# Moving the load and transform steps of batches 1 to 4 in a global filter kernel, and reordering the filter spreads in its opening

## The chip, the cores and the metric

The kernel runs on one core of a Trainium2 chip. The engines of the core work side by side and wait for each other through semaphores: TensorE (matrix multiplies; PE in the profile, PEld for its weight loads), VectorE (DVE), ScalarE (ACT), GpSimd (POOL) and SyncE (SP), which here only issues DMA transfers. The metric is the device time of one execution in microseconds. Each engine executes its instructions in the order in which the program issued them, so an instruction that waits holds all that stand behind it on that engine.

## The reference

Eight batches of 3072 rows by 256 columns go through a global filter (a real FFT along the rows, a product with a complex filter, the inverse FFT), and every resulting row through a small network of two matrices, a maximum and an output matrix.

```python
X = np.fft.rfft(x, axis=1)               # x: 8 x 3072 x 256
Y = X * (filt_r + 1j * filt_i)[None]     # 1537 x 256 each
y = np.fft.irfft(Y, n=3072, axis=1)
h1 = y @ w1                              # 256 x 1024
h2 = y @ w2
out = np.maximum(h1, h2) @ w_out         # 1024 x 256
```

## The kernel before

**The transform.** 3072 is split into 128 times 24. Stage f1 multiplies x with a table of 128 points (`C1`) into `at`. That goes out to DRAM (`ad`) and comes back in another order as `bt`. Stage f2 works in eight groups: it multiplies `bt` with the table `U` (px, L469), multiplies the result with the filter `F` on VectorE (pq, L474) and transforms back with `VP` and `VQ` (pz, L447). ScalarE copies pz into `zt`, and each pair of groups goes to DRAM as `zd` by two writes (L456). `z_read` brings `zd` back as `zr` in two halves (L429), and `s4` multiplies `zr` with `G1` (py, L580) into `yt`, the rows that the network takes.

**The network.** The maximum of two products is computed as the relu of a difference plus the second: `moe_h` multiplies with `Wd`, which is w1 - w2 (L610), and clips the result, mostly on ScalarE. `moe_o` multiplies with `M`, which is w2 times w_out (L630), and adds the clipped part times `Wo` (L635). There are 48 tiles of 512 rows, six for each batch. Half a megabyte goes out for each tile through POOL's queue (L642).

**Folded loads.** From batch 2 on, x is loaded in six pieces a batch, each by two DMAs on SP's queue (`load_p`, L395). Two POOL operations (`fold_x`, L402) add and subtract the halves of a piece into `xd`. `f1_half` (L410) transforms a piece and issues its write of `ad` on SP. The eight reads of `f1_read` (L423) then bring the batch back as `bt`. All DMAs of loads, `ad`, `bt`, `zd` and `zr` are issued on SP, in the order of the program: an issue that waits holds the later ones.

**The order of the work.** The main loop at the end has 48 tiles of eight steps each; step `8 * tt + j` issues `moe_h(tt, j)`, then `moe_o(tt - 1, j)`, then what the dictionary `todo` holds for this step, in the order in which it was planned, and in one step of each tile `s4(tt + 1)`: in its fifth step (j = 4), but in the last tile of a batch at j = 6 (of the first batch at j = 7). `plan` fills `todo`: `plan_f2(n, steps, z1, z0)` gives the nine calls of f2 for batch n and the steps of its two z reads, and `plan_x(n, steps)` gives the loads of batch n and, 12 steps later, the folds. `spaced` makes rows of steps. So the numbers in these calls are a timetable written by hand. The generator `gen_f2(b)` also holds f1 of the next batch: `units` names the calls that begin with an `f1_half`. For batch 1 these are the third to the eighth, which start with piece 3; for the others the first, second, fourth, fifth, seventh and eighth, which start with piece 0. The `zd` writes are issued in the third, fifth, seventh and ninth call. `in_f2` names steps in which ScalarE takes all clippings; outside of them VectorE takes those of j = 1 and j = 5.

**The opening.** Before the loop, batch 0 is transformed without the way through DRAM, while the tables and the filter are made. `expand_f(g, ri, E)` spreads the filter's rows of group `g` (`ri` 0 the real part, 1 the imaginary) over the partitions: eight matmuls with `Sel` (L131, L134), and copies into `F` by engine `E`. On VectorE these are two copies (L141) out of two banks of the "px" ring, which has four; on ScalarE one copy (L514) out of a double bank of the "pa" ring, which has two and is used by `first_s1`, pz and pw as well. `first_t1` (L505) transposes a group of f1's result, `first_s2` (L521, L530) makes its products with `F`, of which in five rounds ScalarE and POOL make one of the two, and `first_s3` (L548) transforms back, two rounds later. `fix_f` (L306, L307) is three POOL operations that put the rows of frequency zero into group 0, after the DMAs of `patch_f0`. `order` is the order of the groups: 1, 2, 3, 4, 5, 0, 6, 7.

Of the kernel before, what the change touches and what calls it, by code (L numbers as in the profile page):

```python
# [29 lines left out]
def kernel(  # L30
# [26 lines left out]
    V, S, G, TE = nc.vector, nc.scalar, nc.gpsimd, nc.tensor  # L57
# [30 lines left out]
    def bank2(shape, dtype, name, tag=None):  # L88
        if tag is None:
            ring.append(ring.pop(0))  # L90
            tag = ring[-1]
        return p2.tile(shape, dtype, tag=tag, name=name)
# [5 lines left out]
    def load_x(b, c):  # L98
        t_ = xpool.tile([128, 4, D], BF16, tag="xb", name="xb")
        src = x[b].rearrange("(p n) d -> p n d", n=N2)  # L100
        G.dma_start(out=t_, in_=src[:, 4 * c:4 * c + 4, :])
        xb[b, c] = t_
# [17 lines left out]
    def expand_f(g, ri, E, sp=0):  # L120
        if E is V:
            pf = [p2.tile([128, 2, D], FP32, tag="px", name="pf", bufs=4) for _ in range(2)]
        else:
            p_ = bank2([128, 2, 2, D], FP32, "pf")
            pf = [p_[:, b] for b in range(2)]
        fs = Fs[ri]
        spin(pf[0].rearrange("p u d -> p (u d)"), sp)
        for b in range(2):
            for c in range(2):
                m = 4 * b + c  # L130
                TE.matmul(pf[b][64 * c:64 * c + 32], Sel[:, m], fs[:, 2 * g:2 * g + 2], start=True, stop=True)  # L131
                p0 = 64 * c + 32
                if g:
                    TE.matmul(pf[b][p0:p0 + 32], Sel[:, 7 - m], fs[:, 16 - 2 * g:14 - 2 * g:-1], start=True, stop=True)  # L134
                else:
                    TE.matmul(pf[b][p0:p0 + 32, 0], Sel[:, 7 - m + c], fs[:, 0], start=True, stop=True)
                    TE.matmul(pf[b][p0:p0 + 32, 1], Sel[:, 7 - m], fs[:, 15], start=True, stop=True)
        f_ = F[:, ri, :, 2 * g:2 * g + 2].rearrange("p b u d -> p b (u d)")
        if E is V:
            for b in range(2):  # L140
                V.tensor_copy(f_[:, b], pf[b].rearrange("p u d -> p (u d)"))  # L141
        else:
            evac(E, f_, p_.rearrange("p b u d -> p b (u d)"))
# [142 lines left out]
    def table_e(t1):  # L286
        V.tensor_scalar(t1, pid, 12.0, None, OP.is_equal)
        V.tensor_scalar(e0[:, 0:1], pid, 0.0, t1, OP.is_equal, OP.add)
        V.tensor_scalar(e0[:, 1:2], e0[:, 0:1], -1.0, 1.0, OP.mult, OP.add)
        V.tensor_scalar(e0[:, 0:1], e0[:, 0:1], -0.5, 1.0, OP.mult, OP.add)  # L290
# [13 lines left out]
    def fix_f():  # L304
        for ri in range(2):
            G.tensor_scalar(F[0:64, ri, 0, 0], F0[:, ri, 0], e0[0:64, ri:ri + 1], None, OP.mult)  # L306
        G.tensor_copy(F[0:64, :, 1, 0], F0[:, :, 1])  # L307
# [14 lines left out]
    def tables_q(h, E):  # L322
        pw = bank2([128, 2, 512], FP32, "pw")
        for k in range(2):
            TE.matmul(pw[:, k], SW, VP[:, 8 * h + 4 * k:8 * h + 4 * k + 4], start=True, stop=True)
        evac(E, VQ[:, 8 * h:8 * h + 8].rearrange("p u b n -> p (u b n)"), pw.rearrange("p k n -> p (k n)"))
# [9 lines left out]
    def spin(pd, n):  # L336
        for _ in range(n):
            TE.matmul(pd, Sp, Sp.rearrange("p (o x) -> p o x", o=1).to_broadcast([128, 4, 128]), start=True, stop=True)  # L338
# [150 lines left out]
    def first_s1(c, E, sp=1):  # L489
        pa = bank2([128, 2, 2, 2, 4, T], FP32, "pa")  # L490
        spin(pa[:, 0].rearrange("p b a n t -> p (b a n t)"), sp)
        for dh in range(2):
            for n in range(4):
                TE.matmul(pa[:, dh, :, :, n], xb[0, c][:, n, 128 * dh:128 * dh + 128],
                          Ct.rearrange("p (b a t) -> p b a t", b=2, a=2), start=True, stop=True)
        evac(E, At[:, :, 0:48].rearrange("p h (a n) t -> p h a (n t)", a=2)[:, :, :, 128 * c:128 * c + 128],
             pa.rearrange("p h b a n t -> p (h b) a (n t)"))

    def first_t1(g, E):
        pt = p2.tile([128, 2, 2, D], BF16, tag="px", name="pt", bufs=4)  # L500
        t0 = 8 * (g // 2) + 2 * (g % 2)
        for c in range(2):
            for i in range(2):
                for dh in range(2):
                    TE.transpose(pt[:, c, i, 128 * dh:128 * dh + 128],  # L505
                                 At[:, 2 * dh:2 * dh + 2].rearrange("p b m t -> p t (b m)")[:, t0 + 4 * c + i], I128)
        o = bt[0][0:ROWS, 8 * (g // 2):8 * (g // 2) + 8].rearrange("p (c u) d -> p c u d", c=2)[:, :, 2 * (g % 2):2 * (g % 2) + 2]
        evac(E, o.rearrange("p c u d -> p c (u d)"), pt[0:ROWS].rearrange("p c u d -> p c (u d)"))

    def evac(E, out_, in_):  # L510
        if E is V:
            V.tensor_copy(out_, in_)
        else:
            S.activation(out_, in_, AF.Copy)  # L514

    def first_s2(g, pool):
        px = [p2.tile([128, 2, D], FP32, tag="px", name="px", bufs=4) for _ in range(2)]
        for i in range(2):
            for k, c in QUADS:
                t_ = 8 * (g // 2) + 4 * c + 2 * (g % 2) + i  # L520
                TE.matmul(px[k][64 * c:64 * c + 64, i], U[64 * k:64 * k + 48, 4 * g + 2 * i + c],  # L521
                          bt[0][64 * k:64 * k + 48, t_], start=True, stop=True)
        if pool:
            xs = apool.tile([128, 2, D], FP32, tag="at", name="xs")
            S.activation(xs[0:FROWS], px[1][0:FROWS], AF.Copy)
        pq = []
        for k in range(2):
            pq.append(pqpool.tile([128, 2, 2, D], BF16, tag="pq", name="pq"))
            E, src = (G, xs) if k and pool else (V, px[k])
            E.tensor_tensor(pq[k][0:FROWS],  # L530
                            src[0:FROWS].rearrange("p (o i) d -> p o i d", o=1).to_broadcast([FROWS, 2, 2, D]),
                            F[0:FROWS, :, k, 2 * g:2 * g + 2], OP.mult)
        return g, pq
# [151 lines left out]
    load_f0()  # L685
    patch_f0()
    first_s1(5, S, 2)
    expand_f(6, 0, V)
    first_t1(1, V)
    first_t1(2, V)  # L690
    expand_f(1, 1, S)
    expand_f(7, 0, S)
    table_e(t1)
    pend = []
    for n, g in enumerate(order):
        pend.append(first_s2(g, n in (0, 1, 2, 4, 6)))
        if n < 6:
            first_t1(order[n + 2], V)
        if n == 0:
            tables_pe()  # L700
            expand_f(2, 1, S)
        if n < 6:
            expand_f((0, 3, 4, 5, 6, 7)[n], 1, S)
        if n < 2:
            load_x(1, 4 + n)
        if n == 2:
            fix_f()
        if n in (1, 3):
            tables_q(n // 2, S)
        if n in (4, 6):  # L710
            prep_wd(n // 2 - 2, *wf)
        if n in (4, 5):
            prep_w(n - 4, V)
        if n > 5:
            prep_w(n - 4, S)
        if n == 5:
            table_g()
        if n > 1:
            first_s3(*pend.pop(0))
# [21 lines left out]
    def plan(step, fn, *a):  # L741
        todo.setdefault(step, []).append((fn, a))

    def plan_x(n, steps, lag=12):
        for c, s_ in enumerate(steps):
            plan(s_, load_p, n, c)
            plan(s_ + lag, fold_x, n, c)

    def plan_f2(n, steps, z1, z0):
        g = []  # L750

        def go():
            if not g:
                g.append(gen_f2(n))
            next(g[0], None)

        for s_ in steps:
            plan(s_, go)
        plan(z1, z_read, n, 1)
        plan(z0, z_read, n, 0)  # L760

    def spaced(first, gap, count):
        return [first + int(gap * i) for i in range(count)]
# [3 lines left out]
    for c in range(4, 12):  # L767
        plan(int(0.6 * (c - 3)), f1, 1, c, (S, V)[c % 2])
    plan(5, f1_read, 1)
    plan_f2(1, spaced(15, 2.4, 9), 28, 36)  # L770
    for c in range(3):
        plan(6 + c, load_p, 2, c)
        plan(7 + 2 * c, fold_x, 2, 3 + c)
        plan(15 + 2 * c, fold_x, 2, c)
    plan(36, f1_read, 2)
    plan_x(3, spaced(24, 3, 6))
    plan_f2(2, spaced(60, 2.5, 9), 74, 81)
    plan(83, f1_read, 3)
    plan_x(4, spaced(64, 3.5, 6))
    plan_f2(3, spaced(104, 3, 9), 121, 129)  # L780
    plan(130, f1_read, 4)
    plan_x(5, spaced(108, 3.5, 6))
    plan_f2(4, spaced(150, 3.3, 9), 168, 178)
    plan(179, f1_read, 5)
    for n in range(5, B):
# [4 lines left out]
        plan_f2(n, spaced(197 + o, 3.4, 9), 216 + o, 226 + o)  # L790

    def in_f2(step):
        return 0 <= step < 6 or 15 <= step < 36 or 60 <= step < 82 or 104 <= step < 130

    for tt in range(6 * B + 1):
        b, i = divmod(tt, 6)
        for j in range(8):
            step = 8 * tt + j
# [38 lines left out]
```

## Time and profile before

| what | value |
| --- | --- |
| median of 9 runs | 527.6 us (524.67 to 528.65) |
| the profiled execution: its time, its span | 526.93 us, 525.2 us |
| TensorE busy | 510.0 us, 97% of the span |
| ScalarE, VectorE, POOL busy | 336.5, 322.7, 148.5 us |
| longest waits of TensorE for a DMA | `bt` (L469) 2.4 us in two pieces, `zr` (L580) 2.4 us in two |
| granted TensorE clock over the span | 0.997 of full speed |

The page gives the busy time of each engine, a chain of work followed back from the last instruction, the costliest groups of instructions (line, engine, what they write and read, count, busy time, mean duration, idle time before them and what ended it) and the DMA issues. Other views show the same execution as a list of waits (who waited for whom: total, times, longest), as a timeline (start, duration, engine, line, operation; in brackets the idle time before it and what ended it) and as sums over windows of time.

### The profile page before, as it was taken

How to read it: one execution, taken by the hardware profiler on the slowest of the kernel's cores; microseconds unless marked ns; L12 is line 12 of the kernel's file. 1: busy time of each engine (PE TensorE's matmuls, PEld its weight loads, DVE VectorE, ACT ScalarE, POOL GpSimd, SP SyncE). 2: the span in 40 equal slices, each digit the busy share in tenths (PEclk: the TensorE clock that was granted, in tenths of full speed). 3: DMA queues.
4: the chain of work that ended last, by engine and by line, in shares of the span. 5: the costliest groups of instructions: out<-in, count | busy, mean ns of one | idle time of the engine just before them, and what ended most of it. 6: DMA issues, size and time to landing. Idle time of an engine off the chain costs nothing.

```text
span 525.2 us, 12607 instructions
## 1 busy us (share of the span) xinstructions
PE 510.0 (97%) x5282; PEld 346.7 (66%) x5282; DVE 322.7 (61%) x438; ACT 336.5 (64%) x598; POOL 148.5 (28%) x168
## 2 busy tenths in 40 slices
PE   9999989979999999999999999999999999999997
PEld 3556656656666666676667666676667666677775
DVE  8987567535783476537783587537783588544442
ACT  6787659736885588756775577656775566545542
POOL 6684524263128203540066002720000000000000
PEclk9999989999999999999999999999999999999999
DMA  7993897998798969897798859995466935341212
GB/s 143 283 198 98 199 221 225 308 189 190 229 230 245 199 198 305 242 191 188 211 264 204 190 156 254 273 194 148 142 172 156 176 111 144 103 126 41 82 61 101
DMA packets 74093, 97.03 MB, mean 185 GB/s; under 512 B 5106, under 2 KB 49780, under 8 KB 73044
## 3 DMA queue, kind: packets, MB, share of 16 engines
q1 hardware_dynamic: 63012, 63.72, 53.2%
q0 software_dynamic: 11024, 32.51, 20.1%
q8 instruction: 41, 0.67, 0.6%
q14 instruction: 16, 0.13, 0.1%
HBM read 54.79 MB, written 47.19 MB: 194 GB/s over the span
## 4 chain that ended last, share of the span: by engine, by line
PE 85%; DMA 8%; ACT 4%; DVE 1%; issue 1%; SPq 0%; ACTq 0%; DVEq 0%
PE ph L610 30%; PE po L635 29%; PE po L630 7%; PE pz L447 4%; DMA zd<-zt 4%; PE py L580 3%; PE px L469 3%; DMA zr<-zd 2%; PE pa L410 2%; PE pd L338 2%; DMA bt<-ad 1%; ACT F L514 1%; ACT At L514 1%; DMA ad<-at 1%; PE pz L548 1%; PE pf L131 1%
## 5 line engine op out<-in xcount | busy, mean ns | idle before, releaser
L615 ACT ACTIVATE gt<-ph 128x512 bf16<-128x512 f32 x308 | 181.9, 603 | 127.3 <-PE ph L610 126.1
L635 PE MATMUL po<-Wo,gt 128*128 128x256 bf16 x1536 | 230.4, 273 | 0.0
L635 PEld LDWEIGHTS <-gt 128*128 128x128 bf16 x1536 | 150.6, 98 | 58.1 <-issue 0.6
L474 DVE TENSOR_TENSOR pq<-px,F 120x1024 bf16<-120x1024 f32 x112 | 131.8, 1219 | 31.9 <-PE px L469 31.6
L637 DVE COPY ot<-po 128x512 f32<-128x512 f32 x96 | 66.3, 690 | 104.2 <-PE po L635 103.8
L642 POOL DMA_DIRECT2D out_dram<-ot x47 | 25.8, 548 | 321.4 <-DVE ot L637 302.1
L402 POOL TENSOR_TENSOR xd<-xf 128x512 bf16<-128x512 f32 x72 | 89.1, 1269 | 38.0 <-DMA xf<-in_x_dram 27.4
L610 PEld LDWEIGHTS <-Wd 128*128 128x128 bf16 x768 | 70.9, 98 | 21.6 <-issue 13.2
L451 ACT ACTIVATE zt<-pz 112x512 bf16<-112x512 f32 x112 | 60.9, 601 | 17.8 <-PE pz L447 16.4
L613 DVE TENSOR_SCALAR gt<-ph 128x512 bf16<-128x512 f32 x76 | 52.2, 686 | 29.6 <-PE ph L610 23.7
L413 ACT ACTIVATE at<-pa 128x512 bf16<-128x512 f32 x72 | 39.1, 595 | 15.0 <-PE pa L410 14.7
L580 PE MATMUL py<-G,zr 128*128 128x128 bf16 x376 | 29.2, 219 | 2.8 <-DMA zr<-zd 2.4
L580 PEld LDWEIGHTS <-zr 128*128 128x128 bf16 x376 | 24.7, 98 | 5.8 <-issue 4.7
L447 PE MATMUL pz<-pq,VP 56*64 56x256 bf16 x448 | 28.4, 271 | 0.0
L447 PE MATMUL pz<-pq,VQ 56*64 56x256 bf16 x448 | 28.0, 268 | 0.0
L469 PE MATMUL px<-bt,U 48*64 48x256 bf16 x448 | 22.8, 274 | 2.4 <-DMA bt<-ad 2.4
L469 PEld LDWEIGHTS <-U 48*64 48x64 bf16 x448 | 11.5, 106 | 10.5 <-issue 5.3
L530 DVE TENSOR_TENSOR pq<-px,F 120x1024 bf16<-120x1024 f32 x11 | 13.2, 1221 | 3.5 <-ACT F L514 1.9
L410 PE MATMUL pa<-xd,C 64*64 64x512 bf16 x144 | 14.8, 400 | 0.0
L447 PEld LDWEIGHTS <-VP 56*64 56x64 bf16 x448 | 13.5, 105 | 1.8 <-issue 1.7
L514 ACT ACTIVATE F<-pf 128x1024 bf16<-128x1024 f32 x10 | 10.1, 1030 | 6.9 <-PE pf L134 6.9
L447 PEld LDWEIGHTS <-VQ 56*64 56x64 bf16 x448 | 13.3, 106 | 0.0
(389 smaller groups left out, 611.2 us busy)
## 6 DMA issues: line engine op xcount, KB each, us to landing
out_dram<-ot POOLq DMA_DIRECT2D x47, 512.0 KB, 5.1
xf<-in_x_dram SPq DMA_DIRECT2D x72, 256.0 KB
ad<-at SPq DMA_DIRECT2D x42, 256.0 KB
bt<-ad SPq DMA_DIRECT2D x56, 192.0 KB
zd<-zt SPq DMA_DIRECT2D x56, 192.0 KB
zr<-zd SPq DMA_DIRECT2D x14, 768.0 KB
xb<-in_x_dram POOLq DMA_DIRECT2D x12, 256.0 KB, 10.9
wf<-in_moe_w_dram POOLq DMA_DIRECT2D x2, 1024.0 KB, 9.8
```

The costliest lines, as they stand in the source:

```text
L402: G.tensor_tensor(xb[b, c][:, i], xf[:, 0], xf[:, 1], op)
L413: S.activation(at[:, 2 * m:2 * m + 2], pa[m], AF.Copy)
L447: TE.matmul(pz[c][64 * k:64 * k + 64, i], W[64 * c:64 * c + 56, 2 * g + i, k], pq[k][64 * c:64 * c + 56, ri, i], start=(ri == 0), stop=(ri ...
L451: S.activation(zt[0:ROWS, c, o:o + 2], pz[c][0:ROWS], AF.Copy)
L469: TE.matmul(px[k][64 * c:64 * c + 64, i], U[64 * k:64 * k + 48, 4 * g + 2 * i + c], bt_[64 * k:64 * k + 48, t_], start=True, stop=True)
L474: V.tensor_tensor(pq[k][0:FROWS], px[k][0:FROWS].rearrange("p (o i) d -> p o i d", o=1).to_broadcast([FROWS, 2, 2, D]), F[0:FROWS, :, k, 2 ...
L580: TE.matmul(py[:, n], zr[b][:, 4 * i + n, 128 * dc:128 * dc + 128], G1, start=True, stop=True)
L610: TE.matmul(ph, Wd[:, dc, 128 * j:128 * j + 128], y_[:, dc].rearrange("p a b -> p (a b)"), start=(dc == 0), stop=(dc == 1))
L613: V.tensor_scalar(gt[tt][:, j], ph, 0.0, None, OP.max)
L615: S.activation(gt[tt][:, j], ph, AF.Relu)
L635: TE.matmul(p_, g_[:, jj, 128 * n:128 * n + 128], Wo[:, jj], start=False, stop=(jj == 7))
L637: V.tensor_copy(ot[tt][:, n - 1:n + 1], po[tt])
```

## The change

In the opening, the spreads of the filter change places. The real spread of group 6 no longer stands before the T1 tiles; the imaginary spread of group 1 does. The imaginary spread of group 2 follows the two T1 tiles, where the real one of group 7 stood. The imaginary spreads of the groups 3, 4, 5, 0 move one round ahead or three back, and the real spreads of groups 6 and 7 come in rounds 2 and 4. `fix_f` moves from round 2 to round 3.

In the timetable, f2 of batch 1 starts at step 17 instead of 15, with slightly closer calls, and ends at 35 instead of 34. f2 of batch 2 takes steps 58 to 77 instead of 60 to 80. The loads of batches 3, 4 and 5 now start after the preceding batch's z reads and `f1_read` were issued (steps 38, 83 and 132 instead of 24, 64 and 108). The z reads of batch 2 and the `bt` reads of batches 2 and 3 move by one to four steps, and `in_f2` follows.

```diff
     first_s1(5, S, 2)
-    expand_f(6, 0, V)
+    expand_f(1, 1, S)
     first_t1(1, V)
     first_t1(2, V)
-    expand_f(1, 1, S)
-    expand_f(7, 0, S)
+    expand_f(2, 1, S)
     table_e(t1)
...
         if n == 0:
             tables_pe()
-            expand_f(2, 1, S)
         if n < 6:
-            expand_f((0, 3, 4, 5, 6, 7)[n], 1, S)
+            expand_f((3, 4, 5, 0, 6, 7)[n], 1, S)
         if n < 2:
             load_x(1, 4 + n)
-        if n == 2:
-            fix_f()
         if n in (1, 3):
             tables_q(n // 2, S)
+        if n == 2:
+            expand_f(6, 0, V)
+        if n == 3:
+            fix_f()
+        if n == 4:
+            expand_f(7, 0, S)
...
     plan(5, f1_read, 1)
-    plan_f2(1, spaced(15, 2.4, 9), 28, 36)
+    plan_f2(1, spaced(17, 2.25, 9), 28, 36)
     for c in range(3):
         plan(6 + c, load_p, 2, c)
         plan(7 + 2 * c, fold_x, 2, 3 + c)
         plan(15 + 2 * c, fold_x, 2, c)
-    plan(36, f1_read, 2)
-    plan_x(3, spaced(24, 3, 6))
-    plan_f2(2, spaced(60, 2.5, 9), 74, 81)
-    plan(83, f1_read, 3)
-    plan_x(4, spaced(64, 3.5, 6))
+    plan(37, f1_read, 2)
+    plan_x(3, spaced(38, 3, 6))
+    plan_f2(2, spaced(58, 2.4, 9), 70, 78)
+    plan(80, f1_read, 3)
+    plan_x(4, spaced(83, 3, 6))
     plan_f2(3, spaced(104, 3, 9), 121, 129)
     plan(130, f1_read, 4)
-    plan_x(5, spaced(108, 3.5, 6))
+    plan_x(5, spaced(132, 3, 6))
     plan_f2(4, spaced(150, 3.3, 9), 168, 178)
...
-        return 0 <= step < 6 or 15 <= step < 36 or 60 <= step < 82 or 104 <= step < 130
+        return 0 <= step < 6 or 17 <= step < 36 or 58 <= step < 79 or 104 <= step < 130
```

## The prediction

> **What bounds the kernel now.** I read the page first, then who waited for whom on TensorE, then TensorE's timeline around each wait, then the queues (SP, POOL) that feed it.
>
> ```profile
> span 525.2 us, 12607 instructions
> PE 510.0 (97%) x5282; PEld 346.7 (66%) x5282; DVE 322.7 (61%) x438; ACT 336.5 (64%) x598; POOL 148.5 (28%) x168
> PE 85%; DMA 8%; ACT 4%; DVE 1%; issue 1%; SPq 0%; ACTq 0%; DVEq 0%
> ...
> PE px L469 <- DMA bt<-ad: 2.4, 2, 1.5
> PE py L580 <- DMA zr<-zd: 2.4, 2, 2.2
> ```
>
> TensorE is busy for 97%, so only its waits can be won. Two matter, both for a DMA: the first read of `bt[1]` and a read of `zr[1]`. On the timeline (start, duration, what; in brackets the idle time before it):
>
> ```profile
> 65.05 0.29 PE L469 MATMUL px<-bt,U 48*64 48x256 bf16 x1
> 66.83 0.30 PE L469 MATMUL px<-bt,U 48*64 48x256 bf16 x4 [1.49 <-DMA bt<-ad]
> 68.05 0.34 PE L469 MATMUL px<-bt,U 48*64 48x256 bf16 x3 [0.92 <-DMA bt<-ad]
> ...
> 113.61 0.61 PE L580 MATMUL py<-G,zr 128*128 128x128 bf16 x8 [2.20 <-DMA zr<-zd]
> ...
> 240.31 0.41 PE L410 MATMUL pa<-xd,C 64*64 64x512 bf16 x4
> ```
>
> I count by plan steps: a step starts with its pair of L610 matmuls. A quiet step lasts 0.98 us (0.43 of L610, 0.55 of L630 and L635, in the chain's rows), one with `s4` 1.42. Step 15 starts at 63.98 and step 16 at 68.33: 4.35 us where step work and eight px (0.33) need 1.31, so 3.0 lost. Steps 16 and 17 lose 0.9 and 0.7 more (1.89 and 2.54 us, against 0.98 and 1.85 elsewhere), since the clock falls (window; busy time of PE, PEld, DVE, ACT, POOL; clock, DMA share, GB/s):
>
> ```profile
> 64.00:68.20 4.20, 1.79 (x17) 0.91 (x14) 0.69 (x1) 0.83 (x2) 0.63 (x1) 1.00 1.25 152
> 68.20:71.70 3.50, 3.50 (x16) 1.82 (x14) 2.35 (x2) 0.98 (x2) 0.00 (x0) 0.51 1.27 152
> ```
>
> Step 47 (110.27 to 114.68) takes 4.41 where 1.42 would do: 3.0 lost, the clock staying at 1.00. Why `zr[1]` is late stands in SP's queue, and what the x loads do behind it in POOL's:
>
> ```profile
> 97.36 3.50 SPq L395 DMA_DIRECT2D xf<-in_x_dram  x2
> 100.95 1.91 SPq L456 DMA_DIRECT2D zd<-zt  x2
> 107.50 0.48 SPq L429 DMA_DIRECT2D zr<-zd  x1
> 108.08 7.49 SPq L423 DMA_DIRECT2D bt<-ad  x8
> 115.61 3.66 SPq L395 DMA_DIRECT2D xf<-in_x_dram  x4
> ...
> 127.05 4.95 POOL L402 TENSOR_TENSOR xd<-xf 128x512 bf16<-128x512 f32 x4 [13.93 <-DMA xf<-in_x_dram]
> ...
> 218.58 0.89 SPq L456 DMA_DIRECT2D zd<-zt  x2
> 223.57 0.48 SPq L429 DMA_DIRECT2D zr<-zd  x1
> ...
> 453.45 1.75 SPq L456 DMA_DIRECT2D zd<-zt  x2
> 457.60 0.45 SPq L429 DMA_DIRECT2D zr<-zd  x1
> ```
>
> The last `zd` write is ready at about 99.3 but is issued at 100.95 behind an x load, and the `zr` read waits till 107.50 for it to land. From write to read it is 6.5 us here, 5.0 in batch 3, 4.15 in batch 7, where no x load is near. The reader is also to see the other side: an x load issued right behind eight `bt` reads lets its fold start only at 127.05, 19.5 us after the `zr` read's issue.
>
> **The change part by part.** The sum is made against the profiled execution (526.93 us, span 525.2), 0.7 below the median of nine.
>
> **f2(1) from step 15 to 17.** px asks two quiet steps later, at 66.9 instead of 65.0. The piece of `bt` seen at 66.83 has landed; the one seen at 68.05 has not, and five of the eight px cover some 0.3. Left: 0.85 of 3.0, and too little to halve the clock. Gain 2.2+1.6 = **3.8** (ends: 2.2 with the clock still halved, 4.6 with the reads a little earlier).
>
> **Batch 3's x loads from steps 24-39 to 38-53.** Twelve SP issues leave the stretch of f2(1)'s `zd` writes. f2(1) now ends with step 35, one step later. From the end of that step: the write is issued 1.2 later (217.36 to 218.58 in batch 3), the `zr` read 4.15 after it, and it lands after 6.0 (107.50 to 113.48): 11.4. `s4` asks after eleven quiet steps, 0.44 for the `s4` in step 36, and its own step's 0.98: 12.2. The 3.1 of steps 47 and 48 go: gain **3.1** (ends 2.5 and 3.1; what stays of this wait shortens the next one equally).
>
> **What is late next.** Step 58's call begins with `f1_half(3, 0)`, which needs fold 0 of batch 3, and TensorE queues everything behind it. Its loads now stand in SP's queue behind the `zr` read and the eight `bt` reads. From the end of step 35: 1.2 + 4.15 to the `zr` read's issue, 19.5 to the start of the fold, 2.5 for its two POOL operations (1.27 each): 27.4. That row had an output store beside it, so I take 27.0. TensorE asks after steps 36 to 57, which take 99.07 to 125.00 less the 3.1 lost there, and 0.98 of its own: 23.8. Wait: **3.2** (ends: 2.4 with 0.8 less beside the loads; 4.5 with batch 3's 5.0 for write to read). Fold 1 then ends 2.5 after fold 0, as step 60 asks 2.6 later: nothing.
>
> **Batch 4's loads from 64-81 to 83-98.** The same 27.0 after step 77; step 104 asks 26 quiet steps, three `s4` and 0.98 later: 27.7. Covered by 0.7, **0** (end: 1.0). `zr[2]` gets three steps more, so the 0.3 that step 94 loses goes: gain **0.3** (ends 0 and 0.3).
>
> **Batch 5's loads from 108-125 to 132-147.** f2(3) ends at 217.36, f2(4)'s first call (the L410 row at 240.31) stands 22.95 later, and fold 0 needs 27.0: wait **4.1** (ends 3.3 and 5.4). Before, these loads were long done and nothing waited here.
>
> **POOL.** The waiting folds hold the output stores queued behind them (steps 55 and 151) by 8 us; `ot` has two buffers and is next written 12 steps after, against 5.1 us to land. 0 (end 1.0).
>
> **f2 spacing and `in_f2`.** Calls at steps 28 and 60 now meet an `s4` there; such a step lasts 3.02 (198.23 to 201.25) against 2.17+0.44 apart, before only a px call met one at 60. Loss **0.7** (ends 0.1 and 0.8). Of the relus only step 81's moves, ACT to DVE, 0.6 beside idle time. `f1_read(2)` one step later and `f1_read(3)` three earlier have 20 steps of cover: 0.
>
> **Clock.** A wait of 2.65 idle in 3.0 us cost 1.6 more in clock; that of step 47 cost none. 4.1 is beyond both, 3.2 a little beyond: 1.6 for the first, half of it for the second: loss **2.4** (ends 0 and 3.2).
>
> [...]
>
> **Opening.** Ahead of the T1 tiles, `expand_f(6, 0, V)` (0.6 on TensorE, two casts of 0.68 on DVE) gives way to `expand_f(1, 1, S)`, whose bank is free when DVE ends its At eviction (18.65); the T1 copies stay at about 19.7 and 20.3. `expand_f(2, 1, S)` takes the place of `expand_f(7, 0, S)` and needs the 432 KB piece of filt_i, issued at 10.84 and about 9.4 on its way: 20.2, where TensorE stands at 20.0. ACT, which the chain names in most of the stretch from 20.7 to 32, has one eviction less before the first products: gain 0.9. Later, `expand_f(6, 0, V)` adds 1.2 to DVE and two px buffers in round 2, where DVE has gaps of 0.5. `expand_f(7, 0, S)` lands in round 4, where TensorE has no gaps (12.67 busy of 12.9): loss 0.4, and 0.2 as pz gets its bank after one eviction more. `fix_f` a round later waits for the same patch DMA (32.95), the POOL product behind it starts at 35.33 as now: 0. Sum: gain **0.3** (ends: gain 0.9, loss 0.8).
>
> **Sum:** -3.8 -3.1 +3.2 +4.1 -0.3 +0.7 +2.4 -0.3 = +2.9. 526.9+2.9 = 529.8; the step counts are good to some 0.3, and I say **529.5 us**.
>
> **The rivals.**
>
> **Folds in time (the other side, faster).** If the x pieces land without waiting for the `bt` reads, the two waits and the clock's share go: 526.9 -6.8 = 520; with half of them left, 523 to 525. It decides where the two waits and the clock sum to less than 5.9 (526.0): the way from `zr` read to fold must shrink by 1.5, to about 20, which also spares one half-clock stretch. For: every duration in it but one stems from a single passage with a store beside it. Against: the row at 127.05.
>
> **The z reads stay late or the clock stays low at step 17 (the change doesn't do what it says).** Output stores of 512 KB still land among the writes. A rest at step 47 takes as much off step 58, so only the clock, 1.6, and a later fold, some 1, remain: 531 to 532. Against: batch 7 with its 4.15.
>
> **The opening loses.** DVE's copies and the px buffers in round 2 hold pz, TensorE's gapless stretch then starts no earlier: +0.8 instead of -0.3, up to 1.5: about 531.
>
> **How the numbers follow.** Forecast 0.55 (own range 526.5 to 532), folds in time 0.25, z reads or clock 0.1, opening 0.1. About 0.3%, 1.6 us, is what can be told from no change: 526.0 to 529.2. Faster: 0.22 of the second case and 0.03 of the forecast, 0.25. Same: 0.2 of the forecast, 0.03 of the second, 0.02 of the others: 0.25. Slower: 0.5. The range goes from 523.5, which leaves half of the second case out, to 532.5: the upper ends of the two waits without more clock.
>
> **What would show it.** Right: L469 waits once for `bt`, under 1 us, near 67; py waits under 0.7 at step 47; L410 matmuls wait for `xd` some 3 us at step 58 and 4 us at step 150, with the clock at half behind at least one. POOL's folds wait long before both. Wrong: no L410 wait, x loads landing among the `bt` reads, or L410 waiting at step 104 too.

## The result, and the profile after

The changed kernel took 537.55 us (median of 11 runs, 533.55 to 541.63) against 527.88 us for the kernel before (34 runs, 524.67 to 529.79): a ratio of 1.0175, 95% interval [1.0153, 1.0197]. It is 9.7 us **slower**, outside the range of 523.5 to 532.5. The direction was the forecast's; the size was not: +1.9 on the median (+2.9 on the profiled execution).

The first profiled execution of the changed kernel took 541.63 us, the far end of its runs. I read a second one, of 538.25 us (span 536.4), close to the median. Against the profiled execution before (526.93, span 525.2) it is 11.2 us longer in span, of which some 1.6 are the two executions' places in their spreads (0.95 below the one median, 0.7 above the other).

The page of that execution, top lines, the row of granted clocks (40 slices of 13.4 us) and the chain by engine:

```profile
span 536.4 us, 12617 instructions
PE 517.3 (96%) x5282; PEld 350.1 (65%) x5282; DVE 323.3 (60%) x439; ACT 336.8 (63%) x597; POOL 148.3 (28%) x168
PEclk9969999998999999997999999999999999999999
PE 81%; DMA 8%; SPq 4%; ACT 2%; DVE 2%; POOL 1%; issue 1%; POOLq 0%; ACTq 0%
```

TensorE is busy for 517.3 us instead of 510.0 with the same 5282 matmuls: two thirds of the loss are matmuls that take longer (a pair of L610 takes 0.44 us at 124.30, ahead of step 58's wait, and 0.83 at 128.85, behind it, where the granted clock is 0.50), and the clock row shows where, in the third slice (27 to 40 us, the opening), the tenth (121 to 134, step 58) and the nineteenth (241 to 255, step 150). The chain holds DMA for 8% as before, but now 4% for SP's queue (SPq), which had 0%.

Who waited for whom, longest first (total, times, longest, in us):

```profile
PE pa L410 <- POOL xd L402: 6.7, 4, 3.5
PE pt L505 <- ACT xs L525: 1.7, 1, 1.7
PE pf L131 <- ACT At L514: 1.1, 1, 1.1
```

Both waits for a DMA that led the list before, `bt` and `zr`, are gone from its head (in the execution of 541.63 us 1.1 us of the `zr` wait are left). In their place stand the fold wait that the prediction named (6.7 us) and two waits for ScalarE in the opening that it did not. TensorE's timeline around them (start, duration, what; in brackets the idle time before):

```profile
25.91 0.41 PE L521 MATMUL px<-bt,U 48*64 48x256 bf16 x8
27.98 0.67 PE L505 MATMUL pt<-I,At 128*128 128x128 bf16 x8 [1.65 <-ACT xs L525]
...
112.76 0.61 PE L580 MATMUL py<-G,zr 128*128 128x128 bf16 x8
113.83 0.85 PE L610 MATMUL ph<-y__2154,Wd 128*128 128x512 bf16 x2 [0.46 <-ACT y__2154 L583]
...
126.94 0.37 PE L410 MATMUL pa<-xd,C 64*64 64x512 bf16 x1 [1.49 <-POOL xd L402]
128.16 0.41 PE L410 MATMUL pa<-xd,C 64*64 64x512 bf16 x3 [0.85 <-POOL xd L402]
...
247.63 0.37 PE L410 MATMUL pa<-xd,C 64*64 64x512 bf16 x1 [3.54 <-POOL xd L402]
248.86 0.64 PE L410 MATMUL pa<-xd,C 64*64 64x512 bf16 x3 [0.85 <-POOL xd L402]
```

The idle times alone understate the fold waits: the first matmul runs on the sums, the next ones wait for the differences. Step 58 takes 4.55 us and step 150 6.91, where 1.63 would do for either.

The clock in windows (window; busy time of PE, PEld, DVE, ACT, POOL; clock, DMA share, GB/s):

```profile
26.00:29.50 3.50, 1.85 (x32) 1.06 (x32) 2.34 (x4) 2.19 (x4) 3.29 (x3) 1.00 1.20 217
29.50:33.00 3.50, 3.50 (x63) 2.28 (x61) 2.66 (x4) 1.58 (x2) 1.07 (x1) 0.51 1.32 209
...
36.40:39.80 3.40, 3.40 (x34) 1.79 (x31) 1.82 (x2) 2.14 (x4) 2.36 (x2) 0.50 0.84 158
...
128.60:131.90 3.30, 3.30 (x17) 1.59 (x12) 2.95 (x3) 1.74 (x4) 2.92 (x4) 0.50 1.07 239
243.00:248.00 5.00, 1.46 (x10) 0.75 (x8) 0.47 (x1) 0.60 (x1) 1.67 (x2) 1.00 1.05 306
248.00:254.80 6.80, 5.95 (x30) 3.02 (x29) 2.95 (x3) 2.28 (x4) 6.37 (x7) 0.50 1.07 236
```

Half clock follows each of the three waits: for 3.4 us after step 58's, 6.8 after step 150's, and 10.2 (29.54 to 39.78) after the opening's. In the execution of 541.63 us the last one lasted 13.7 (28.74 to 42.4).

Why the folds are late stands in SP's queue:

```profile
226.42 0.47 SPq L429 DMA_DIRECT2D zr<-zd  x1
227.00 7.76 SPq L423 DMA_DIRECT2D bt<-ad  x8
234.88 14.80 SPq L395 DMA_DIRECT2D xf<-in_x_dram  x12
```

and in POOL's rows, whose first fold of batch 5 waited for its load until 246.33, 19.9 us after the `zr` read:

```profile
246.33 2.48 POOL L402 TENSOR_TENSOR xd<-xf 128x512 bf16<-128x512 f32 x2 [7.96 <-DMA xf<-in_x_dram]
```

Step by step against the kernel before, beside the prediction's terms. A stretch's number is how much longer it lasts than before, from the starts of the steps at its ends. The last column is the timetable alone, an experiment below.

| stretch | predicted | changed kernel | timetable alone |
| --- | --- | --- | --- |
| opening, to step 0 | -0.3 | +4.9 | -0.1 |
| steps 0 to 35 (`bt` wait; calls at an `s4`) | -3.8 + 0.4 | -3.4 | -3.2 |
| steps 36 to 51 (`zr` wait) | -3.1 | -2.2 | -2.2 |
| steps 52 to 81 (fold wait, clock, a call at an `s4`) | +3.2 + 0.8 + 0.3 | +4.7 | +3.5 |
| steps 82 to 103 | -0.3 | -0.3 | -0.3 |
| steps 104 to 149 | 0 | 0.0 | +0.3 |
| steps 150 to 153 (fold wait, clock) | +4.1 + 1.6 | +7.6 | +7.7 |
| sum (what is left over: -0.1) | +2.9 | +11.2 | +5.7 |

So 5.2 of the 8.3 us that the prediction missed lie in the opening, 1.9 at step 150, 0.9 at step 47 and 0.4 at step 58.

### The profile page after: what moved, and what is told of

The parts are those of the page before. It is cut to its first block, busy times and chain, and to the rows that moved or that the text cites. A ratio compares the mean times of both kernels' runs of the same rounds, so it can differ in the third digit from the quotient of the medians.

```text
span 539.8 us, 12617 instructions
## 1 busy us (share of the span) xinstructions
PE 518.0 (96%) x5282; PEld 350.4 (65%) x5282; DVE 323.7 (60%) x439; ACT 336.9 (62%) x597; POOL 148.2 (27%) x168
## 3 DMA queue, kind: packets, MB, share of 16 engines
q0 software_dynamic: 11024, 32.51, 19.7%
## 4 chain that ended last, share of the span: by engine, by line
PE 83%; DMA 5%; SPq 4%; DVE 4%; ACT 2%; issue 1%; POOL 1%; POOLq 0%; ACTq 0%; DVEq 0%
PE ph L610 29%; PE po L635 28%; PE po L630 7%; PE pz L447 4%; DMA xf<-in_x_dram 4%; PE py L580 3%; SPq L423 3%; PE px L469 3%; PE pa L410 2%; DMA zd<-zt 1%; PE pf L131 1%; PE pz L548 1%; POOL xd L402 1%; PE pt L505 1%; ACT at L413 1%
## 5 line engine op out<-in xcount | busy, mean ns | idle before, releaser
L610 PEld LDWEIGHTS <-Wd 128*128 128x128 bf16 x768 | 71.1, 98 | 22.0 <-issue 13.2
L413 ACT ACTIVATE at<-pa 128x512 bf16<-128x512 f32 x72 | 39.1, 595 | 24.9 <-PE pa L410 24.3
L580 PE MATMUL py<-G,zr 128*128 128x128 bf16 x376 | 29.5, 219 | 1.8 <-DMA zr<-zd 1.1
L410 PE MATMUL pa<-xd,C 64*64 64x512 bf16 x144 | 16.2, 410 | 8.1 <-POOL xd L402 8.1
L469 PE MATMUL px<-bt,U 48*64 48x256 bf16 x448 | 23.9, 279 | 0.0
L530 DVE TENSOR_TENSOR pq<-px,F 120x1024 bf16<-120x1024 f32 x11 | 13.2, 1220 | 4.8 <-issue 3.8
L410 PEld LDWEIGHTS <-C 64*64 64x64 bf16 x144 | 4.5, 104 | 16.4 <-issue 14.9
```

Source lines behind the costliest of these rows:

```text
L413: S.activation(at[:, 2 * m:2 * m + 2], pa[m], AF.Copy)
L580: TE.matmul(py[:, n], zr[b][:, 4 * i + n, 128 * dc:128 * dc + 128], G1, start=True, stop=True)
L610: TE.matmul(ph, Wd[:, dc, 128 * j:128 * j + 128], y_[:, dc].rearrange("p a b -> p (a b)"), start=(dc == 0), stop=(dc == 1))
```

## The experiments

Two theories stood at the start. **A:** the opening loses by itself, through the new wait in round 2 and the half clock behind it, and the timetable loses 3 to 6 us through the folds. **B:** the opening is innocent and all of it lies in the timetable, through the folds and their clock.

### The changed kernel again

> The changed kernel once more, for a second look at its profile. If the half clock in the opening belongs to the change, TensorE waits again some 1.7 us at a T1 tile of round 2 (L505) for ScalarE, the clock is at half for at least two windows of 3.4 us before step 0, and step 0 starts after 51 us (before: 48.3). If it was chance in the first profile, step 0 starts at 48 to 49. Either way L410 waits for the folds at steps 58 and 150, about 3 and 5 us.

This is the execution shown above: 538.25 us. The half clock in the opening and both fold waits are there as in the first profile, so they are no accident of that one execution; their lengths differ (step 0 at 53.27 and 54.91, against 48.33 before). Not every execution need have all of it: over the runs of this kernel the mean granted clock went from 0.978 to 0.994, and 0.994 is also what the timetable alone shows, below, with nothing lost in its opening.

### The opening alone

The opening of the change with the timetable of before:

```diff
-    expand_f(6, 0, V)
+    expand_f(1, 1, S)
     first_t1(1, V)
     first_t1(2, V)
-    expand_f(1, 1, S)
-    expand_f(7, 0, S)
+    expand_f(2, 1, S)
...
-            expand_f(2, 1, S)
...
+        if n == 2:
+            expand_f(6, 0, V)
...
+        if n == 4:
+            expand_f(7, 0, S)
```

> Only the opening of the change, with the timetable of before. Theory A (the opening costs much of the loss, through a wait of TensorE in round 2 and the half clock that follows): 530 to 535 us, step 0 after 51 us. Theory B (all of the loss is in the timetable; the half clock in the opening was chance): 527 to 529 us, step 0 at 48 to 49.

It took 531.6 us, ratio 1.0055 [1.0024, 1.0085]. B falls: the opening loses with the old timetable, too. Of what A expected, the wait is there, but in this execution neither the half clock behind it nor a step 0 after 51: it comes at 50.11, 1.8 later than before. TensorE's timeline in round 2, in this kernel and (the two rows after the dots) in the kernel before, and then ScalarE's in this kernel:

```profile
26.02 0.41 PE L521 MATMUL px<-bt,U 48*64 48x256 bf16 x8
28.09 0.69 PE L505 MATMUL pt<-I,At 128*128 128x128 bf16 x8 [1.65 <-ACT xs L525]
...
26.89 0.41 PE L521 MATMUL px<-bt,U 48*64 48x256 bf16 x8
27.23 0.73 PE L505 MATMUL pt<-I,At 128*128 128x128 bf16 x8
```

```profile
25.61 1.02 ACT L514 ACTIVATE F<-pf 128x1024 bf16<-128x1024 f32 x1 [0.16 <-PE pf L134]
26.53 1.02 ACT L514 ACTIVATE VQ<-pw 128x1024 bf16<-128x1024 f32 x1
27.43 0.60 ACT L525 ACTIVATE xs<-px 120x512 f32<-120x512 f32 x1
```

The T1 transposes of round 2 wait for ScalarE to read a px tile that was written 2 us earlier in the same round. They need its bank. The program's allocation shows it: in the changed opening the second px tile of round 2 and that round's T1 tile lie in the same bank; before, the T1 tile had the bank of a px tile of the round before, which VectorE had long read. In neither program do the "px" banks go round in a fixed order, so moving a spread elsewhere changed which bank this tile gets. ScalarE reads the second px tile only after two other evictions, F and VQ.

Of the 5.3 us by which this execution's span (530.5) is longer than before, only 1.8 are there at step 0; 1.7 are won back at steps 15 to 17, and steps 47 to 49 lose 5.1. There the `zr` wait is 5.2 us instead of 2.2, with half clock behind it (0.994 granted over this execution's span): the last `zd` write, issued at 101.29, let the `zr` read go only at 110.03, 8.7 us later (before: 6.5). Why the write landed later is not settled by these runs; the opening with the mended T1 tile, below, shows the same in a smaller size (a `zr` wait of 4.0 us), so it is not the bank's doing.

Here the clock stayed at 1.00 behind the same wait:

```profile
29.50:39.80 10.30, 9.56 (x211) 5.72 (x203) 8.45 (x11) 8.24 (x10) 7.49 (x6) 1.00 1.09 191
```

### The timetable alone

The opening of before with the whole new timetable:

```diff
-    plan_f2(1, spaced(15, 2.4, 9), 28, 36)
+    plan_f2(1, spaced(17, 2.25, 9), 28, 36)
...
-    plan_x(3, spaced(24, 3, 6))
+    plan_x(3, spaced(38, 3, 6))
...
-    plan_x(5, spaced(108, 3.5, 6))
+    plan_x(5, spaced(132, 3, 6))
```

> Only the timetable of the change, with the opening of before. Theory A: 531 to 534 us, that is 3 to 6 us lost to the folds of steps 58 and 150 less what steps 15 and 47 gain. Theory B: 536 to 538 us, all of the loss. Both: L410 waits for the folds, 3 to 4 us at step 58 and 5 to 6 at step 150, the clock at half after each; the first px of f2(1) waits under 0.5 us.

533.03 us, ratio 1.0093 [1.0058, 1.0129]. The waits list is led by the folds:

```profile
PE pa L410 <- POOL xd L402: 7.9, 4, 4.7
```

That is the time theory A gave. Up to step 52 this kernel is 5.4 us ahead of the one before (113.27 against 118.69): the two z and `bt` waits are won. Steps 52 to 81 give 3.5 of it back and steps 150 to 153 take 7.7. The clock behind the wait of step 58 stayed at 1.00 here, behind that of step 150 it was half from 241.5 to 248.3. By the ratios the opening alone costs 2.9 us and the timetable alone 4.9, together 7.8 of the whole change's 9.7. What is missing fits the half clock in the opening, which of these three profiles only that of the whole change shows. The runs without a profile say that the opening alone has it, too, at times: in four of its ten the mean granted clock was 0.984 to 0.987, in the others 0.994 to 0.997, and the difference is about that of 10 us at half clock (an estimate: half of 10 us is 0.009 of 530).

### The timetable with the x loads at their old steps

```diff
-    plan_x(3, spaced(38, 3, 6))
+    plan_x(3, spaced(24, 3, 6))
...
-    plan_x(4, spaced(83, 3, 6))
+    plan_x(4, spaced(64, 3.5, 6))
...
-    plan_x(5, spaced(132, 3, 6))
+    plan_x(5, spaced(108, 3.5, 6))
```

> The timetable of the change, but with the loads of batches 3, 4 and 5 at their steps of before (from 24, 64 and 108), and the opening of before. If the moved loads make the loss in the timetable: no wait of L410, the wait of zr at step 47 back to some 3 us, the gain at step 17 (some 4 us) kept: 523 to 526 us. If the closer f2 calls or the earlier z reads cost instead: 528 us or more.

533.38 us, ratio 1.0102 [1.0075, 1.0129]: missed by 7 us. The fold waits are gone, but the other side came back larger than it was:

```profile
PE py L580 <- DMA zr<-zd: 6.1, 1, 6.1
PE pz L447 <- DVE pq L474: 1.6, 2, 0.8
```

```profile
99.87 1.05 SPq L456 DMA_DIRECT2D zd<-zt  x2
107.85 0.48 SPq L429 DMA_DIRECT2D zr<-zd  x1
```

With f2 of batch 1 two steps later and the x loads among its `zd` writes, the last write is issued at 99.87 and needs 8.0 us, where it needs 3.8 when no x load is near (97.06 to 100.82 in the timetable alone). Step 47 then takes 8.5 us and the clock falls behind it (0.990 granted over this execution's span). So the moved loads do what the prediction said of them, and a little more; it is their new place that costs. Another 3.8 us are lost from step 110 on, the second row of the waits list, with the clock at half from 197.7 to 201.1. There a fold of batch 4 held POOL's queue until 189.0, two output stores behind it went out late, and VectorE's copy into `ot` waited 4.5 us for a store to land and held its products:

```profile
193.46 0.69 DVE L637 COPY ot<-po 128x512 f32<-128x512 f32 x1 [4.51 <-DMA out_dram<-ot]
```

### Batch 5's loads back, all else of the timetable kept

```diff
-    plan_x(5, spaced(132, 3, 6))
+    plan_x(5, spaced(108, 3.5, 6))
```

> The timetable of the change with the opening of before, and of the timetable only batch 5's x loads back at steps 108 to 125, the timetable alone having taken 533.0 us with an excess of 7.9 us at steps 150 to 152 (6.4 of it the L410 wait and what clings to it, 1.5 the clock). Theory (the wait is the place of these loads in SP's queue, behind the z read and the eight bt reads): the L410 wait at step 150 is gone, that of step 58 stays at about 3.0; 533.0 - 7.9 = 525, between 523.5 and 527. Rival (step 110 pays instead, as it did with all x loads back, 3.8 us with pz waiting for pq): 528 to 530. If the place of the loads has nothing to do with it: 533.

523.78 us, ratio 0.9938 [0.9912, 0.9965]: steps 150 to 153 last as before (1.64, 0.99, 0.97, 2.31), and step 110 does not pay. One line of the timetable carried some 8 us (1.0093 to 0.9938): without it, the rest of the timetable is a gain. L410 still waits at step 58, which takes 3.74: 2.1 over, where 3.0 was expected.

### The first two x pieces ahead of the `bt` reads

```diff
-    plan(37, f1_read, 2)
-    plan_x(3, spaced(38, 3, 6))
+    plan_x(3, (36, 37, 41, 44, 47, 50))
+    plan(38, f1_read, 2)
...
-    plan(130, f1_read, 4)
-    plan_x(5, spaced(132, 3, 6))
+    plan_x(5, (129, 130, 135, 138, 141, 144))
+    plan(131, f1_read, 4)
```

> The timetable of the change with the opening of before, and the first two x pieces of batches 3 and 5 issued behind the z read but ahead of the eight bt reads, which then start one step later (38 and 131 instead of 37 and 130). Theory (folds wait because the eight bt reads, 7.5 to 8.8 us of SP's issuing, stand ahead of the x loads): the fold starts about 13 us after the z read's issue instead of 21, no L410 wait above 0.5 at steps 58 and 150, no clock lost there; 533.0 - 3.0 - 7.9 = 522, between 520.5 and 525, the bt reads landing 4 to 5 us later and still ahead of the first px call. Rival (the transfers share the bandwidth, so that whatever goes second is late): px waits for bt or py for zr by 2 to 4 us instead, 526 to 530.

523.4 us, ratio 0.9921 [0.9894, 0.9949]. SP's queue, and the fold that it feeds:

```profile
101.05 0.47 SPq L429 DMA_DIRECT2D zr<-zd  x1
101.63 3.57 SPq L395 DMA_DIRECT2D xf<-in_x_dram  x4
105.25 9.43 SPq L423 DMA_DIRECT2D bt<-ad  x8
```

```profile
110.65 4.94 POOL L402 TENSOR_TENSOR xd<-xf 128x512 bf16<-128x512 f32 x4 [0.50 <-DMA xf<-in_x_dram]
```

The fold starts 9.6 us after the `zr` read instead of 20.3 (100.82 to 121.09 in the timetable alone), and L410 no longer waits at either step. It is the order in the queue, not the amount that is moved: from the `zr` read to the end of the last of the twenty issues behind it SP needs 22.8 us here and 23.0 in the timetable alone. The `bt` reads, issued 3.6 us later, keep nobody waiting: the one wait of px for `bt` on the list, 0.7 us, is that of step 17, ahead of all this. Step 164 pays 0.5 that the kernel before does not: VectorE's copy into `ot` waits 2.35 us for an output store, which stood behind folds in POOL's queue. The rival, that whatever goes second is late by 2 to 4 us, falls.

### The T1 tile of round 2 ahead of the round's products

The opening of the change, the timetable of before, and one thing more:

```diff
+        if n == 2:
+            first_t1(order[n + 2], V)
         pend.append(first_s2(g, n in (0, 1, 2, 4, 6)))
-        if n < 6:
+        if n < 6 and n != 2:
             first_t1(order[n + 2], V)
```

> The opening of the change with the timetable of before, and in round 2 alone the T1 tile is transposed ahead of the round's first products instead of behind them, so that it gets another bank than the products have just used. The opening of the change alone took 531.6 us and came to step 0 at 50.11 in its profile (before: 48.33). Theory (the 1.65 us wait of the T1 transposes in round 2 is for the bank, whose reader on ScalarE stands behind two other evictions): the L505 wait for ScalarE is gone, step 0 at 48.5 to 49.0, 528 to 530 us. Rival (ScalarE is the bound of the stretch whatever the bank, and the wait moves to the next matmul that needs it): step 0 at 50 again, 531 to 532 us.

528.77 us, ratio 1.001 [0.9988, 1.0032]: no difference to before that can be told, against 1.0055 without this edit. The T1 tile now gets a bank that neither px tile of the round uses, and TensorE goes on without a stop:

```profile
25.45 0.61 PE L325 MATMUL pw<-VP,SW 128*128 128x512 bf16 x2
25.89 0.66 PE L505 MATMUL pt<-I,At 128*128 128x128 bf16 x8
26.49 0.41 PE L521 MATMUL px<-bt,U 48*64 48x256 bf16 x8
```

ScalarE's rows have the same times as above to 0.04 us, with the same order F, VQ, xs. So ScalarE was no bound there; the bank was. Step 0 comes at 48.80, 0.5 later than before.

### The same mend in the whole change

The whole change with the edit of the last experiment and nothing else.

> The whole change, and of the two mends only that of the opening: the T1 tile of round 2 ahead of the round's first products. The change as it is took 537.55 us, with step 0 at 53.3 and 54.9 in its two profiles and the clock at half for 10 to 14 us before it. Theory (the bank wait of 1.65 us sets off the half clock in the opening): step 0 near 48.9, no half clock before it, the waits of 3 and 5 us at steps 58 and 150 with their clock unchanged; 537.55 - 4.4 to - 6 = 531.5 to 533.2, as the timetable alone (533.0). Rival (the half clock comes from the whole stretch being thin, with the wait or without): it stays, and the gain is the 1.3 of open_t1 alone, 536.

532.43 us, ratio 1.0098 [1.0072, 1.0123]: 5.1 us less than the change as it is by the medians, 4.1 by the ratios, and level with the timetable alone (533.03). Step 0 comes at 48.86, and the clock row has no slice below 9 before the nineteenth, which holds step 150:

```profile
PEclk9999999999999999997999999999999999999999
```

The mean granted clock was 0.994 in all four runs; it was lower in all but one run of the change. One wait of 1.65 us for a bank and the half clock behind it were 4 to 5 of the 9.7 us.

### Passing the wait at step 150 with work

The timetable alone, and TensorE is given matmuls on constants while it waits; their results are overwritten.

```diff
         pa = [ps.tile([128, 2, D], FP32, tag="ps", name="pa") for _ in range(2)]
+        if (b, c) == (5, 0):
+            for _ in range(27):
+                TE.matmul(pa[0], Wo[:, 0, 0:128], Wo[:, 0:2], start=True, stop=True)
```

> The timetable of the change with the opening of before, and at step 150 TensorE passes the wait for the fold with 27 matmuls of 512 columns on constants (5.75 us at full clock by 0.213 each), whose results are overwritten. The wait itself stays as long; only what follows it can change. In the timetable alone step 150 took 8.05 us, 151 and 152 1.90 and 1.53, with the clock at half from 241.5 to 248.3. Theory (the idle wait sets off the half clock, which costs 1.5 behind the wait and some 0.9 inside step 150): step 150 at 7.1 to 7.5, steps 151 and 152 at 0.99 and 0.98, 533.0 - 2 = 531. Rival (the clock falls by itself there, or the matmuls on constants delay the fold's reader): steps 151 and 152 as before, 533 to 534.

530.7 us, ratio 1.0058 [1.0039, 1.0076] against 1.0093: 1.8 us less, by doing more. The two intervals overlap a little, so that the clock and the steps have to carry the reading. Three lines are added ahead of it, so L410 is L413 here, and so on:

```profile
239.19 5.99 PE L411 MATMUL pa<-Wo 128*128 128x512 bf16 x27
245.11 0.41 PE L413 MATMUL pa<-xd,C 64*64 64x512 bf16 x4
```

```profile
241.00:245.00 4.00, 4.00 (x20) 1.68 (x18) 0.00 (x0) 0.00 (x0) 2.53 (x3) 1.00 1.06 279
245.00:247.00 2.00, 2.00 (x22) 1.16 (x22) 1.22 (x2) 1.44 (x3) 2.00 (x2) 1.00 1.06 234
```

The clock stays at 1.00, and steps 151 and 152 take 0.99 and 0.98 instead of 1.90 and 1.53. Steps 150 to 153 together take 11.74 us instead of 13.65, though the matmuls on the fold come as late after the start of step 150 in both (6.9 and 7.1 us: the 27 matmuls took 5.92, 0.219 each, and ran 1.8 us past the end of the fold, at 243.35 by POOL's row, so that the last of them were themselves a delay). So 1.7 of the 1.9 us are the clock's, and at this wait it is the idleness of TensorE that set it off: the clock was 0.50 from 241.5 to 248.3 with TensorE idle in the wait, and 1.00 from 237 to 250 with it busy. The runs without a profile agree: the mean granted clock was 0.996 to 1.000 in all nine, and 0.990 to 0.994 in the four of the timetable alone. In this execution step 58's wait, which had no such filling, was followed by half clock (step 59 took 1.90), where it was not in the timetable alone: that part comes and goes.

### Both mends, and the version kept

The whole change with the T1 edit and with the x pieces of batches 3 and 5 ahead of the `bt` reads:

> The whole change with both mends: the T1 tile of round 2 ahead of the round's first products, and the first two x pieces of batches 3 and 5 ahead of the bt reads. If the opening's bank and the queue order carry the loss of the change: step 0 near 48.8, no L410 wait above 0.5 and the clock at half nowhere; 522 to 525 us, faster than before by 0.5 to 1%. If what is left of the opening's cost (the later At wait, 0.5, or a lasting half clock) is separate from the bank: 525 to 530.

523.76 us, ratio 0.993 [0.9904, 0.9956]; no L410 wait on the list, no half clock (1.000 granted over the span), step 0 at 49.01, and step 164 1.2 over, behind a copy into `ot` that waits 3.1 us for its store. The opening as changed still gains nothing. So the last version takes the opening of before, the new timetable with batch 3's first two x pieces ahead of the `bt` reads, and batch 5's loads at their old steps:

```diff
-    plan_f2(1, spaced(15, 2.4, 9), 28, 36)
+    plan_f2(1, spaced(17, 2.25, 9), 28, 36)
...
-    plan(36, f1_read, 2)
-    plan_x(3, spaced(24, 3, 6))
-    plan_f2(2, spaced(60, 2.5, 9), 74, 81)
-    plan(83, f1_read, 3)
-    plan_x(4, spaced(64, 3.5, 6))
+    plan_x(3, (36, 37, 41, 44, 47, 50))
+    plan(38, f1_read, 2)
+    plan_f2(2, spaced(58, 2.4, 9), 70, 78)
+    plan(80, f1_read, 3)
+    plan_x(4, spaced(83, 3, 6))
```

with `in_f2` as in the change.

> The opening of before; of the timetable the later f2(1) and the moves of batches 3 and 4, but the first two x pieces of batch 3 ahead of the bt reads, and batch 5's x loads left at steps 108 to 125. If the gains of the mends add: no L410 wait above 0.5 at steps 58 and 150, no px wait for bt behind step 100 (0.7 in x_first), span 520 to 521.5, 522.5 to 523.5 us, 0.8 to 1.1% faster than before. If x loads among batch 4's z writes cost as they did at step 110 with all x loads back: 525 to 527.

521.93 us, ratio 0.990 [0.988, 0.992]: 1.0% faster than the kernel before, and a little below the time expected. Step 164 costs nothing here. Of the waits of TensorE that remain, the longest that is for a DMA of the loop is one of 0.5 us for `bt` (at step 17), and L410 waits once, 0.4, at step 104, which takes 0.8 more than before. From the list:

```profile
PE pd L338 <- DVE Sp L167: 1.1, 1, 1.1
...
PE px L469 <- DMA bt<-ad: 0.5, 1, 0.5
PE pa L410 <- POOL xd L402: 0.4, 1, 0.4
```

## Why the prediction was right or wrong

**f2(1) from step 15 to 17: right.** Predicted -3.8, with 0.4 back for the call that meets an `s4` at step 28 (3.02 us, as said): -3.4, measured -3.4. The `bt` wait at step 17 is too short to head the list.

**Batch 3's x loads and the `zr` wait: right in kind, 0.9 too large.** The wait is gone, but the step lost 3.0 us before and gained 2.2. The row shown had the answer: `py` stood idle for 2.20, not 3.0. The other 0.8 is not the DMA's: the next step needs the `y` that this very `s4` makes, and waits for its eviction (the row at 113.83, idle 0.46, from L583), with or without a late `zr`. I took the price from the length of the step, where the idle time before the row gave the wait itself.

**The fold wait at step 58: right.** Predicted 3.2; step 58 is 2.9 over in the changed kernel, 3.0 in the timetable alone. The way was as worked out: 1.2 to the last `zd` write, 4.1 to the `zr` read (101.79 to 105.91), then 19.7 to the fold (19.1 predicted). That the size fits is in part luck: the 0.9 us that stayed at step 47 made TensorE ask later than the sum had it, and the 0.6 that the fold came later made up for most of it.

**The fold wait at step 150: mechanism right, too small.** Predicted 4.1; step 150 is 5.3 over in the changed kernel and 6.4 in the timetable alone, of which 0.4 in either is half clock behind the wait, within the step. The term that was mis-sized is the way from the `zr` read to the fold. I took it as one number, 19.1, from a single passage of before; in five executions with the x loads behind the reads it was 19.0 to 21.0 us at step 150. The rival "Folds in time", which needed it to shrink, had its condition on the wrong side. The experiment that put two x pieces ahead of the reads brought it to 8.6 (9.6 at step 58).

**The clock behind the fold waits: mechanism right, too small.** Predicted 1.6 at step 150, and half of that at step 58. Behind step 150 it cost 2.3 us (steps 151 to 153 take 0.90, 0.94 and 0.44 more), plus the 0.4 inside step 150; filling the wait saved 1.9. At step 58 it cost some 1.3 in the changed kernel and nothing in the timetable alone, so that half a price was a fair mean and wrong each time. The trace of before had shown one stretch of half clock, of 3.4 us (it cost 1.6); here it lasted 6.8. The clock fell behind the idle gap of 3.54 us at step 150, but also behind gaps of 1.49 and 0.85 (step 58) and of 1.65 (the opening), and it stayed at 1.00 behind the same 1.65 in the opening alone: in these executions the length of the gap did not tell whether the clock would fall. The trace of before already had both: the prediction gives 2.65 us idle for the first of its two waits, but the rows have 2.4 (1.49 and 0.92), with half clock behind it, and 2.20 for the second, with the clock at 1.00 behind it.

**Batch 4's loads at step 104: right.** Predicted 0; 0.0 in the changed kernel, 0.3 in the timetable alone, and 0.8 to 0.9 at step 104 in two later kernels, the end of the bound being 1.0. **POOL's stores**, also put at 0 with an end of 1.0, cost TensorE nothing in the changed kernel, but 0.5 to 3.8 us in three of the variants above: there the folds held a store so long that the next copy into `ot` waited for it.

**The opening: wrong, and the largest miss.** Predicted -0.3, with ends -0.9 and +0.8; measured +4.9 (+1.8 where the clock held). What failed is the step on "`expand_f(6, 0, V)` adds 1.2 to DVE and two px buffers in round 2, where DVE has gaps of 0.5". I counted the px buffers as a ring and asked only whether VectorE had time. The gain that I named was there: round 2's products start at 26.02 instead of 26.89, the 0.9 predicted. But the T1 tile behind them had been given the bank of the px tile that ScalarE reads last. (Ahead of the T1 tiles the prediction also named the wrong reader: `expand_f(1, 1, S)` waited 1.1 us for ScalarE's At eviction, not VectorE's, but started within 0.1 us of the 18.65 it gave.) A cost of 1.65 us came from a tile that the change does not touch. The rival "The opening loses" had the sign, but for another reason (VectorE's copies and the px buffers holding pz), and neither it nor the range had the half clock, which made 1.8 into 4.9. No opening term had a clock in it, although the prediction charged one for waits of TensorE in the loop.

## What to carry to other kernels

A late transfer is moved, not removed: before a load is put behind others in a queue, add up the way from that queue's slot to the first instruction that needs the data, and put the piece that is needed first ahead of the ones that can wait. Here two pieces ahead of eight reads turned a loss of 1% into a gain of 0.8%. When allocations in a shared pool change their order, look up which bank each later tile gets: a reader far down another engine's queue can hold a tile that the edit never mentions, here for 1.65 us.

And a stall of TensorE was not priced by its length alone here: what followed at half clock cost 2.7 of the 7.6 us at steps 150 to 153, and 1.3 us or nothing on top of the 2.9 at step 58, and the range has to hold both.

## What was not expected of the hardware

The clock after a wait differed between executions with the same wait. After the same 1.65 us idle gap in the opening (1.85 us busy in the 3.5 us from 26.0 to 29.5 in both) it stayed at 1.00 in the opening alone, and fell to half for 10.2 us in the whole change (13.7 in its first profiled execution, behind a gap of 1.65 again). Step 58 shows the same: TensorE was busy for 1.96 of the 4.30 us from 124.3 to 128.6 in the whole change, and the clock was 0.50 in the 3.3 us behind; it was busy for 2.08 of the 4.62 us from 119.58 to 124.2 in the timetable alone, and the clock was 1.00 in the 4.2 us behind. On what it turned was not shown.

Nor was it shown what sets how long half clock lasts: 3.4 us behind step 58, 6.8 behind step 150, 10.2 and 13.7 in the opening, with TensorE busy for 5.95 us of the 6.8 and for 13.53 of the 13.7.

SP's issues of x loads took longer behind the eight `bt` reads: four took 2.6 to 3.8 us right behind the `zr` read, twelve took 13.2 to 15.8 us behind the `bt` reads, 1.1 to 1.3 each against 0.65 to 0.95.
